# Other operation times in a planner: GpSimd's shifts, some of VectorE's operations, and when products of shifted copies count as ready

## The chip, the core and the metric

The kernel runs on one core of a Trainium2 chip. A core has a matrix engine (TensorE, PE in the profile), a vector engine (VectorE, DVE), an engine for activation functions (ScalarE, ACT), a general one (GpSimd, POOL) and one that issues transfers (SyncE, SP). Each works off its own instructions in the order of the program and waits on semaphores for the others. The metric is the device time of one execution in microseconds (us); of several executions the median is taken.

## The reference

Two attention layers over the same shapes (2048 positions, 512 channels, 32 heads of 16) stand side by side in the output: columns 0 to 511 are A, columns 512 to 1023 are B. Inputs are bfloat16.

```python
def _A_ref(x, wqkv, wo):          # linear attention
    q, k, v = qkv[0], qkv[1], qkv[2]            # of x @ wqkv, 32 heads of 16
    phi = lambda t: jnp.where(t > 0, t + 1, jnp.exp(t)) + 1e-6
    pq, pk = phi(q), phi(k)
    kv = jnp.einsum("bhsd,bhse->bhde", pk, v)
    z = jnp.einsum("bhsd->bhd", pk)
    num = jnp.einsum("bhqd,bhde->bhqe", pq, kv)
    den = jnp.einsum("bhqd,bhd->bhq", pq, z)[..., None] + 1e-6
    o = num / den
    return (lambda x, *d: x.transpose(*d))(o, 0, 2, 1, 3).reshape(B, S, D) @ wo

def _B_ref(x, wqkv, wo):          # softmax attention
    q, k, v = qkv[0], qkv[1], qkv[2]
    scale = Dh ** -0.5
    scores = jnp.einsum("bhqd,bhkd->bhqk", q, k) * scale
    p = _softmax(scores, axis=-1)
    o = jnp.einsum("bhqk,bhkd->bhqd", p, v)
    return (lambda x, *d: x.transpose(*d))(o, 0, 2, 1, 3).reshape(B, S, D) @ wo
```

Nearly all the work is B's 32 heads x 2048 x 2048 exponentials and the products on both sides of them.

## The kernel before

**Units and blocks.** B's work is cut into 32 units: four groups of eight heads, four chunks of 512 queries, and the even or the odd four heads of the group. In a unit, four heads lie in four row groups of TensorE. A unit has 64 blocks; a block is one head's scores of 128 keys by 512 queries, one product (line 809) with 32 rows. In all that makes 2048 blocks. The products of probabilities and values (line 1129) go to one PSUM bank, pPV, in four column groups of 17 columns (16 of the head, and one of ones for the sum); only one unit can have that bank at a time. When its last product is done, VectorE transposes the bank to OT (line 1229), takes the reciprocal of the sums (line 1240) and multiplies (line 1234).

**Two paths for a block.** A block goes through one of two paths.
- ScalarE: the scores stand in pS (five banks), two or three blocks together; one exponential (line 1010) writes PT, and one product per block follows.
- VectorE: the scores stand in pD (two banks, or one lent by pS). VectorE writes a 16-bit integer DI (line 911) whose bits, read as a float16, are a coarse exponential. Two shifted copies DJ are made of it (line 1081), each by adding a constant, by GpSimd or now and then by VectorE; a shift is for up to two blocks (1024 columns). The three copies, times values scaled by 1, 0.797 and 0.633 (the VV copies, line 625), add up to a finer exponential: three products per block, one from DI and two from DJ.

**A's work and the projections.** A's linear attention (88 jobs) and the projections of B's later groups are jobs of a few stages each (matrix products in a free pD bank, then VectorE, sometimes ScalarE). In A's phi, ScalarE writes the exponential EA (line 638), VectorE bounds it (line 647) and adds the positive part (line 640).

**What sets the order.** The kernel is written by a planner that runs while the kernel is built. It holds a clock for each engine (`T`) and a list of what could go next with its ready time and a cost in us written out in the code; again and again it takes what could start earliest, with priorities for near ties, moves that engine's clock by the cost, and adds the instruction to that engine's program. The costs leave no trace in the program but the order, the choice of path for a block, and the choice of engine for a shift; waits on the chip are by semaphores. The names that matter here:
- `d_pick` decides whether a block goes to VectorE: not if VectorE's planned queue is over `DBL` = 4.0 us, or GpSimd's over `PBL` us. GpSimd's queue is reckoned in `p_backlog`: its clock, and a cost for each shift that is still to come. Blocks that it doesn't take are left for ScalarE.
- `shift_cand` plans a shift: for GpSimd at `dp`, for VectorE at `dd`, both linear in the columns. VectorE is taken where GpSimd would end over `LM` us later. There are ten DJ buffers.
- `pv_cand` plans the products with values. A product may start when its probabilities are ready by the plan (`x[0]`; `x[2]` is 0 for PT and DI, 1 or 2 for the shifted copies); they go out in rounds of up to four, two rounds at once at most. `VHI` raises their priority when 24 are outstanding.
- `v4_job`, `phi_stages` and `unit_done` hold the stages with costs that the change touches (the VV copies, A's phi, the end of a unit).
- A's jobs have ready times spread evenly over the kernel, each moved by up to `JIT` = 6 us by a fixed hash of its number and `SEED`.
- `fill_idle` puts idle matmuls on FZ where the plan leaves TensorE idle over 0.25 us (eight in this kernel).

Of the kernel before, what the change touches and what calls it, by code (L numbers as in the profile page):

```python
# [12 lines left out]
ALU = mybir.AluOpType  # L13
# [222 lines left out]
def bass_concat_heads__linear_attn_block__softmax_full_mha__prompt_kernel(nc, A_x, A_wqkv, A_wo, B_x, B_wqkv, B_wo, out):  # L236
# [14 lines left out]
    UB = NT * 4  # L251
    PVB = 8
    PVW = 0.3
    NPP = 2
    DNEXT = 8
    DEND = 12
# [5 lines left out]
    ALAG = 30.0  # L262
    DLEAD = 0.8
    DBL = 4.0
    PBL = 8.0
    SHL = ("pool", "pool")
    LM = 4.0
    FU = 0.6
    SEED = 11
    JIT = 6.0  # L270
    LATE = 0.2
    DBAL = 1
# [17 lines left out]
    with es:  # L290
        block = es.enter_context(nc.Block())

        def sb(name, shape, dt):
            return es.enter_context(nc.sbuf_tensor(name, shape, dt))
# [20 lines left out]
        EA = sb("EA", [128, 2, 512], BF)  # L315
        OT = sb("OT", [128, 2, 512], F32)
        XN = OT.bitcast(BF)[:, 1, :].rearrange("p (x n) -> p x n", n=512)
        ZR = sb("ZR", [128, 2, 16], F32)
# [135 lines left out]
        tok = {}  # L454
# [54 lines left out]
        def f_op(lane, fn, reads=(), writes=()):  # L509
            return lambda bk: sch.add(lane, fn, reads=reads, writes=writes)  # L510
# [11 lines left out]

        def halves(fn, reads, n=4, parts=NPP, dur=MM, after=None, kind="f"):

# [84 lines left out]
        def v4_job(t4, Gp, lane="pool", **kw):  # L609
            sl = Gp % 2  # L610
            def mm(e, bk, i):
                tl, cc = divmod(i, 4)
                t = 4 * t4 + tl
                return e.matmul(f32v(bk)[:, tl * 128:(tl + 1) * 128], lhsT=xTb[:, cc, t * 128:(t + 1) * 128],
                                rhs=Wb[:, cc, 1024 + Gp * 128:1024 + Gp * 128 + 128], start=(cc == 0), stop=(cc == 3))
            ts = range(4 * t4, 4 * t4 + 4)
            def load_wo():
                load(WOb, wob, [("Wb", 2)])
            st = halves(mm, [("Wb", 2)] + [("xTb", t) for t in ts], n=16, parts=NPP, dur=0.06, after=load_wo if (t4, Gp) == (3, NGP - 1) else None)
            vv = lambda k: VV[:, sl, k, 4 * t4:4 * t4 + 4, :].rearrange("p t c -> p (t c)")  # L620
            st.append(("dve", 0.6, f_ev("dve", lambda e, bk: e.tensor_copy(  # L621
                VV[:, sl, 0, 4 * t4:4 * t4 + 4, :].rearrange("p t (h c) -> p t h c", c=17)[:, :, :, 0:16],
                f32v(bk).rearrange("p (t h d) -> p t h d", t=4, d=16)), [], [("VV", t, sl, 0) for t in ts])))
            for k in (1, 2):
                st.append((lane, 0.5 if lane == "dve" else 0.65, f_op(lane, lambda e, k=k: e.tensor_scalar(  # L625
                    vv(k), vv(0), SW[k], 0.0, op0=ALU.mult, op1=ALU.add),
                    [("VV", t, sl, 0) for t in ts] + [("VV1", sl)], [("VV", t, sl, k) for t in ts])))
            needs = ["WbV"] + [("xTb", t) for t in ts] + ([("pvdone", Gp - 2)] if Gp >= 2 else [])
            return Job(st, needs, [(k, ("V", Gp, t, k)) for k in range(3) for t in ts], rel=0, **kw)
# [4 lines left out]
        def phi_stages(x, ea, keys):  # L634
            q = ectr[0] % 2
            ectr[0] += 1
            E = ea(EA[:, q, :])
            ex = f_op("act", lambda e: e.activation(E, x, ACTF.Exp), keys, [("EA", q)])  # L638
            ex.buf = ("EA", q)
            add_ = f_op("dve", lambda e: e.scalar_tensor_tensor(x, x, 0.0, E, op0=ALU.max, op1=ALU.add),  # L640
                        [("EA", q)] + keys, keys)
            def last(bk):
                add_(bk)
                give_back(("EA", q), T["dve"])
            return [
                ("act", 0.52, ex),
                ("dve", 0.48, f_op("dve", lambda e: e.tensor_scalar(EA[:, q, :], EA[:, q, :], 1.0, 1e-6, op0=ALU.min, op1=ALU.add),  # L647
                                  [("EA", q)], [("EA", q)])),
                ("dve", 1.07, last)]

        def akv_job(t, hp, **kw):
            n = 4 * hp + t // 4
# [5 lines left out]
            def after():  # L658
                next_xa(n)
                if hp == 1 and t == NT - 1:  # L660
                    load(WOa, woa, ["WaV"])
            st = halves(mm, ["Wa", "WaV", ("xTa", n % 2)], n=8, parts=NPP, dur=0.11, after=after if t % 4 == 3 else None, kind="v")
            st.append(("dve", 0.6, f_ev("dve", lambda e, bk: e.tensor_copy(KV[:, t, 2:514],
# [170 lines left out]
        pend = []  # L834
# [10 lines left out]

        def p_backlog(at):
            w = max(0.0, T["pool"] - at) + sum(c_[3] for c_ in cands["pool"])
            w += 1.07 * len(pend)
            for s_ in dgroup["st"].values():
                if not s_.get("chained"):  # L850
                    w += 1.07 * len(s_["items"])
            return w

        def lagging(at):
# [208 lines left out]
        def shift_cand():  # L1063
            if not pend:
                return None
            buf, k, n, w, I, items, t_ = pend[0]
            jb = jn[0] % NDJ
            if jfree[jb] is None:
                return None
            dp, dd = 0.1 + w * 0.00095, 0.1 + w * 0.00045  # L1070
            sp, sd = max(T["pool"], vis("dve", t_), jfree[jb]), max(T["dve"], t_, jfree[jb])
            tp = sp + sum(c_[3] for c_ in cands["pool"]) + dp * len(pend)
            td = sd + sum(c_[3] for c_ in cands["dve"]) + dd
            ln, st_, d_ = ("dve", sd, dd) if tp > td + LM else ("pool", sp, dp)
            def run(st_, en_):
                pend.pop(0)
                jn[0] += 1
                jfree[jb] = None
                jleft[jb] = n
                J = DJ[:, jb, 0:w]  # L1080
                sch.add(ln, lambda e: e.tensor_scalar(J, I, 1.0, float(SH[k]), op0=ALU.mult, op1=ALU.add),  # L1081
                        reads=[("DI", buf, i) for i in range(n)], writes=[("DJ", jb)])
                for i, b in enumerate(items):
                    pv_ready[b[0]].append((vis(ln, en_), b, k, DJ.bitcast(F16)[:, jb, i * 512:(i + 1) * 512], ("DJ", jb), ("j", jb)))
                free_di(buf, vis(ln, en_))
            return st_, 0, ln, d_, run, None, "f"
# [4 lines left out]
        def pv_cand():  # L1091
# [1 line left out]
            if u >= NU or pvopen[0] is None:  # L1093
                return None
            Gp, c, e_ = unit(u)
            at = lambda x: max(x[0], tok[("V", Gp, x[1][1], x[2])])
            lst = [x for x in pv_ready[u] if ("V", Gp, x[1][1], x[2]) in tok]
            if not lst:
                return None
# [2 lines left out]
            if not rd:  # L1102
                x = min(lst, key=at)
# [13 lines left out]
            if len(rounds[0]) < 4 and not final and len(rd) < 8 and streaming(t_) > UT:  # L1117
                t_ += PVW
            def make(rounds):
# [102 lines left out]
        def unit_done(u, t_):  # L1222

            if u == NU - 1:
                return last_unit_done(u, t_)
            xb = (u // 2) % 2
            Gp, c, e_ = unit(u)
            lease("OT", 1)
            sch.add("dve", lambda e: e.transpose(OT[:, 0, :], PVb[:, 0:512]), reads=[("PV", g) for g in range(4)], writes=[("OT", 0)])  # L1229
            pvopen[0] = vis("dve", t_)  # L1230
            o = OT[:, 0, :].rearrange("p (b r) -> p b r", r=32)
            xn = XN[:, xb, :].rearrange("p (b r) -> p b r", r=32)
            zr = ZR[:, 0, 0:16]
            mul = f_op("dve", lambda e: e.tensor_tensor(xn[:, :, 16 * e_:16 * e_ + 16], o[:, :, 0:16],  # L1234
                                                        zr.unsqueeze(2).broadcast_to([128, 16, 16]), op=ALU.mult),
                       [("OT", 0), ("ZR", 0)], [("XN", xb, e_)])
            def norm(bk):
                mul(bk)
                give_back("OT", 0.0)
            st = [("dve", 0.2, f_op("dve", lambda e: e.reciprocal(zr, o[:, :, 16]), [("OT", 0)], [("ZR", 0)])),  # L1240
                  ("dve", 0.72, norm)]
            if e_ == 1:
                k = 4 * Gp + c
                st.append(("dve", 0.65, f_op("dve", lambda e: e.transpose(ON[:, k, :], XN[:, xb, :]), [("XN", xb, 0), ("XN", xb, 1)], on_keys(k))))
            urgent.append(Job(st, [("ot", u - 1)] if u else [], [(1, ("ot", u))] + ([(2, ("on", Gp, c))] if e_ == 1 else []),
                              bank=False, ready=t_, prio=0.5))
            if Gp == NGP - 1 and e_ == 1:
                for tl in range(4):
                    urgent2.append(omm_job("b", 4 * c + tl, tl, [("on", Gp, c)], [(-1, ("st", c, tl))]))
# [122 lines left out]
        while True:  # L1372
            opts = []
            for eng in T:
                best = None
                for c_ in cands[eng]:
                    st = max(T[eng], c_[0])
# [37 lines left out]
            o = min((o for o in opts if o[0] <= t0 + 0.03), key=lambda o: (o[1], o[0], -o[3]))  # L1415
            st, _, eng, dur, run_, c_, kind = o
# [25 lines left out]
        last = {}  # L1442
# [77 lines left out]
```

## Time and profile before

| | |
|---|---|
| median of three runs | 726.06 us (723.94 to 726.2) |
| the profiled execution | 725.82 us, span 723.8 us |
| granted clock of TensorE | 0.991 |
| busy: TensorE, ScalarE | 669.3 us, 680.5 us |
| busy: GpSimd, VectorE | 645.7 us, 641.1 us |
| exponentials (line 1010) | 654 instructions, 666.6 us |
| shifts (line 1081) | 581 on GpSimd, 39 on VectorE |

The span runs from the first to the last instruction on the core. A group's row in the profile gives line, engine, operation, output and input tile, shape and count, then busy time and the mean length of one in ns, then the time that its engine stood idle ahead of it and what ended most of that. A row of waits gives who waited, for whom, the time in all, how many times, and the longest. In a row of the timeline stand start and length in us, the instruction and, in brackets, the idle time ahead of it. Instructions of one engine may overlap in the records, so that a mean length can be over the time from start to start.

### The profile page before, as it was taken

What the parts mean: (1) busy time and instruction counts of PE and PEld (TensorE: products, weight loads), DVE (VectorE), ACT (ScalarE), POOL (GpSimd) and SP (SyncE); (2) the same over time, 40 slices, a digit from 0 to 9 for tenths busy, and PEclk for the clock granted to TensorE, in tenths of its full rate; (3) what the DMA queues carried; (4) which work ended last, traced back from release to release, by engine and by line L of the source; (5) the groups of instructions that cost most, each with busy time, mean ns of one, the idle gap of its engine ahead of it and who ended that gap; (6) DMA issues with size and microseconds to landing.
All of it is one profiled execution on the core that took longest, in us unless ns stands there. A gap on an engine that the chain in (4) does not pass through costs nothing.

```text
span 723.8 us, 19047 instructions
## 1 busy us (share of the span) xinstructions
PE 669.3 (92%) x8128; PEld 210.6 (29%) x8128; DVE 641.1 (89%) x1037; ACT 680.5 (94%) x692; POOL 645.7 (89%) x630
## 2 busy tenths in 40 slices
PE   7999999989998999899989998999988989899996
PEld 4323322323332333322222232222222222222222
DVE  6998899989997999888988988888999878989975
ACT  5899999989998998999999999999999999999995
POOL 7699999998999999989988999989999887999994
PEclk9999999999999999999999999999999999999999
DMA  9500011101001101020011001021000100021101
GB/s 208 143 2 2 9 30 32 37 9 39 2 2 31 31 2 31 1 68 12 13 31 37 16 1 30 3 59 38 8 9 9 38 24 31 1 38 31 30 31 34
DMA packets 54508, 21.75 MB, mean 30 GB/s; under 512 B 45200, under 2 KB 53904, under 8 KB 54416
## 3 DMA queue, kind: packets, MB, share of 16 engines
q1 hardware_dynamic: 53360, 20.20, 12.0%
q8 instruction: 66, 1.08, 0.6%
q10 hardware_dynamic: 1056, 0.26, 0.2%
q14 instruction: 26, 0.21, 0.1%
HBM read 4.19 MB, written 4.19 MB: 12 GB/s over the span
## 4 chain that ended last, share of the span: by engine, by line
POOL 49%; DVE 17%; PE 16%; ACT 12%; issue 4%; DMA 1%; DVEq 0%; POOLq 0%
POOL DJ L1081 47%; ACT PT L1010 12%; DVE DI L911 10%; PE pPV L1129 6%; PE pS L809 5%; PE pD L516 3%; POOL VV L625 2%; DVE OT L1229 1%; PE pS L516 1%; DVE DJ L1081 1%; DMA xTb<-in_B_x_dram 1%; DVE EA L647 1%; DVE PQT L640 1%; DVE VV L621 1%; PE pD L809 0%
## 5 line engine op out<-in xcount | busy, mean ns | idle before, releaser
L1010 ACT ACTIVATE PT<-pS 128x1024 f16<-128x1024 f32 (+1 forms) x654 | 666.6, 1180 | 28.9 <-PE pS L809 14.1
L1081 POOL TENSOR_SCALAR DJ<-DI 128x1024 int16<-128x1024 int16 (+1 forms) x581 | 622.5, 1073 | 65.9 <-DVE DI L911 19.2
L911 DVE TENSOR_SCALAR DI<-pD 128x512 int16<-128x512 f32 (+1 forms) x469 | 314.2, 688 | 38.7 <-PE pD L809 31.8
L809 PE MATMUL pS<-QT,KM 32*128 32x512 bf16 x1570 | 258.9, 386 | 14.6 <-ACT PT L1010 12.2
L1129 PE MATMUL pPV<-DJ,VV 128*17 128x512 f16 x1234 | 245.6, 386 | 24.3 <-POOL DJ L1081 23.0
L1129 PE MATMUL pPV<-PT,VV 128*17 128x512 f16 x1431 | 255.7, 385 | 1.6 <-DVE OT L1229 1.6
L809 PE MATMUL pD<-QT,KM 32*128 32x512 bf16 x478 | 171.4, 386 | 2.1 <-DVE DI L911 1.4
L1129 PE MATMUL pPV<-DI,VV 128*17 128x512 f16 x617 | 154.9, 385 | 2.3 <-DVE OT L1229 2.2
L809 PEld LDWEIGHTS pS<-QT,KM 32*128 32x128 bf16 x1570 | 63.9, 91 | 245.3 <-ACT PT L1010 179.5
L911 DVE TENSOR_SCALAR DI<-pS 128x512 int16<-128x512 f32 x139 | 93.9, 676 | 4.6 <-PE pS L809 3.7
L1129 PEld LDWEIGHTS pPV<-DJ,VV 128*17 128x17 bf16 x1234 | 52.1, 88 | 96.7 <-POOL DJ L1081 59.9
L1129 PEld LDWEIGHTS pPV<-PT,VV 128*17 128x17 bf16 x1431 | 53.1, 88 | 49.1 <-issue 41.5
L809 PEld LDWEIGHTS pD<-QT,KM 32*128 32x128 bf16 x478 | 40.6, 91 | 17.6 <-DVE DI L911 10.0
L1129 PEld LDWEIGHTS pPV<-DI,VV 128*17 128x17 bf16 x617 | 32.4, 88 | 24.8 <-issue 15.4
L516 PE MATMUL pD<-Wa,xTa 128*32 128x256 bf16 x896 | 34.8, 277 | 0.7 <-DVE DI L911 0.7
L516 PE MATMUL pD<-xTb,Wb 128*32 128x512 bf16 x432 | 31.3, 383 | 0.3 <-DVE DI L911 0.2
L1081 DVE TENSOR_SCALAR DJ<-DI 128x1024 int16<-128x1024 int16 x39 | 30.7, 791 | 0.0
L1229 DVE STREAM_TRANSPOSE OT<-pPV 128x512 f32<-128x512 f32 x31 | 21.9, 706 | 2.5 <-PE pPV L1129 2.5
L1234 DVE TENSOR_TENSOR OT<-OT,ZR 128x256 bf16<-128x256 f32 x31 | 23.5, 759 | 0.6
L516 PEld LDWEIGHTS pD<-Wa,xTa 128*32 128x32 bf16 x896 | 20.3, 97 | 12.8 <-issue 7.8
L520 DVE CAST KV<-pD 128x512 bf16<-128x512 f32 x24 | 16.4, 682 | 7.6 <-PE pD L516 7.6
L647 DVE TENSOR_SCALAR EA<-EA 128x512 bf16<-128x512 bf16 x32 | 22.3, 698 | 0.3 <-ACT EA L638 0.2
(109 smaller groups left out, 395.3 us busy)
## 6 DMA issues: line engine op xcount, KB each, us to landing
out_dram<-KV SPq DMA_DIRECT2D x32, 128.0 KB, 1.7
KM<-KR SPq DMA_DIRECT2D x96, 16.0 KB, 1.8
Wa<-in_A_wqkv_dram SPq DMA_DIRECT2D x1, 1024.0 KB, 6.1
Wb<-in_B_wqkv_dram SPq DMA_DIRECT2D x2, 384.0 KB, 4.5
Wb<-in_B_wqkv_dram SPq DMA_DIRECT2D x1, 512.0 KB, 4.7
Wa<-in_A_wqkv_dram SPq DMA_DIRECT2D x1, 512.0 KB, 6.8
Wa<-in_A_wo_dram SPq DMA_DIRECT2D x1, 512.0 KB, 5.0
Wb<-in_B_wo_dram SPq DMA_DIRECT2D x1, 512.0 KB, 3.8
```

What stands on the lines that cost most here:

```text
L516: ins = e.matmul(out[32 * g:32 * g + 32], lhsT=lhsT[:, 32 * g:32 * g + 32], rhs=rhs, start=start, stop=stop, tile_position=(0, 32 * g))
L520: return lambda e, bk: (e.tensor_copy(out_fn(), in_fn(bk)) if lane == "dve" else e.activation(out_fn(), in_fn(bk), ACTF.Copy))
L621: st.append(("dve", 0.6, f_ev("dve", lambda e, bk: e.tensor_copy(VV[:, sl, 0, 4 * t4:4 * t4 + 4, :].rearrange("p t (h c) -> p t h c", c=17 ...
L625: st.append((lane, 0.5 if lane == "dve" else 0.65, f_op(lane, lambda e, k=k: e.tensor_scalar(vv(k), vv(0), SW[k], 0.0, op0=ALU.mult, op1=A ...
L647: ("dve", 0.48, f_op("dve", lambda e: e.tensor_scalar(EA[:, q, :], EA[:, q, :], 1.0, 1e-6, op0=ALU.min, op1=ALU.add), [("EA", q)], [("EA", ...
L809: return e.matmul(dst, lhsT=KM[32 * g:32 * g + 32, Gp % 2, e_, j * 128:(j + 1) * 128], rhs=QT[32 * g:32 * g + 32, Gp % 2, c * 512:(c + 1) ...
L911: sch.add("dve", lambda e: e.tensor_scalar(DI[:, buf, i * 512:(i + n) * 512], f32v(DBANK[bi], 512 * n), ESC, EB, op0=ALU.mult, op1=ALU.add ...
L1010: sch.add("act", lambda e: e.activation(PT[:, row, c0:c0 + w], SCR[sl][:, 0:w], ACTF.Exp, scale=SC), reads=skeys(sl)[:len(bl)], writes=[(" ...
L1081: sch.add(ln, lambda e: e.tensor_scalar(J, I, 1.0, float(SH[k]), op0=ALU.mult, op1=ALU.add), reads=[("DI", buf, i) for i in range(n)], wri ...
L1129: sch.add("pe", lambda e, g=g, j=j, h=h, k=k, P=P, first=first, last_=last_: e.matmul(PVb[32 * g:32 * g + 17, 0:512], lhsT=VV[:, Gp % 2, k ...
L1229: sch.add("dve", lambda e: e.transpose(OT[:, 0, :], PVb[:, 0:512]), reads=[("PV", g) for g in range(4)], writes=[("OT", 0)])
L1234: mul = f_op("dve", lambda e: e.tensor_tensor(xn[:, :, 16 * e_:16 * e_ + 16], o[:, :, 0:16], zr.unsqueeze(2).broadcast_to([128, 16, 16]), ...
```

## The change

Only numbers of the planner change, and one condition: in `pv_cand` a product of a shifted copy counts as ready half a microsecond (`PVM`) after the copy. Planned operations: the shift on GpSimd (1024 columns: 1.073 us to 1.130 us) and on VectorE (0.561 to 0.701), the VV copies (VectorE 0.5 to 0.4, GpSimd 0.65 to 0.71), A's phi on VectorE (0.48 to 0.64 and 1.07 to 1.25), the reciprocal and the multiplication at a unit's end (0.2 to 0.26, 0.72 to 0.68). The limits `PBL` (8.0 to 6.5) and `LM` (4.0 to 5.0) and the number `SEED` (11 to 8) change too.

```diff
+    PVM = 0.5
...
-    PBL = 8.0
+    PBL = 6.5
     SHL = ("pool", "pool")
-    LM = 4.0
+    LM = 5.0
     FU = 0.6
-    SEED = 11
+    SEED = 8
...
-                st.append((lane, 0.5 if lane == "dve" else 0.65, f_op(lane, lambda e, k=k: e.tensor_scalar(
+                st.append((lane, 0.4 if lane == "dve" else 0.71, f_op(lane, lambda e, k=k: e.tensor_scalar(
...
-                ("dve", 0.48, f_op("dve", lambda e: e.tensor_scalar(EA[:, q, :], EA[:, q, :], 1.0, 1e-6, op0=ALU.min, op1=ALU.add),
+                ("dve", 0.64, f_op("dve", lambda e: e.tensor_scalar(EA[:, q, :], EA[:, q, :], 1.0, 1e-6, op0=ALU.min, op1=ALU.add),
                                   [("EA", q)], [("EA", q)])),
-                ("dve", 1.07, last)]
+                ("dve", 1.25, last)]
...
         def p_backlog(at):
             w = max(0.0, T["pool"] - at) + sum(c_[3] for c_ in cands["pool"])
-            w += 1.07 * len(pend)
+            w += 1.13 * len(pend)
             for s_ in dgroup["st"].values():
                 if not s_.get("chained"):
-                    w += 1.07 * len(s_["items"])
+                    w += 1.13 * len(s_["items"])
...
-            dp, dd = 0.1 + w * 0.00095, 0.1 + w * 0.00045
+            dp, dd = 0.157 + w * 0.00095, 0.22 + w * 0.00047
...
-            at = lambda x: max(x[0], tok[("V", Gp, x[1][1], x[2])])
+            at = lambda x: max(x[0] + (PVM if x[2] else 0.0), tok[("V", Gp, x[1][1], x[2])])
...
-            st = [("dve", 0.2, f_op("dve", lambda e: e.reciprocal(zr, o[:, :, 16]), [("OT", 0)], [("ZR", 0)])),
-                  ("dve", 0.72, norm)]
+            st = [("dve", 0.26, f_op("dve", lambda e: e.reciprocal(zr, o[:, :, 16]), [("OT", 0)], [("ZR", 0)])),
+                  ("dve", 0.68, norm)]
```

## The prediction

> **What bounds the kernel now.** I read the page's busy times and the chain of waits first, then the groups with shapes kept apart, then who waited for whom on each engine, and last short timelines. Busy time of the engines and the chain that ended last, from the page:
>
> ```profile
> span 723.8 us, 19047 instructions
> PE 669.3 (92%) x8128; PEld 210.6 (29%) x8128; DVE 641.1 (89%) x1037; ACT 680.5 (94%) x692; POOL 645.7 (89%) x630
> POOL 49%; DVE 17%; PE 16%; ACT 12%; issue 4%; DMA 1%; DVEq 0%; POOLq 0%
> ```
>
> Four engines are busy for about nine tenths of the span, and the chain changes from one to the other; half of it is GpSimd. The groups that the change prices or moves (count, busy us, mean ns of one, idle before):
>
> ```profile
> L1010 ACT ACTIVATE PT<-pS 128x1024 f16<-128x1024 f32 (+1 forms) x654 | 666.6, 1180 | 28.9 <-PE pS L809 14.1
> L1129 PE MATMUL pPV<-PT,VV 128*17 128x512 f16 x1431 | 255.7, 385 | 1.6 <-DVE OT L1229 1.6
> L1129 PE MATMUL pPV<-DI,VV 128*17 128x512 f16 x617 | 154.9, 385 | 2.3 <-DVE OT L1229 2.2
> L1129 PE MATMUL pPV<-DJ,VV 128*17 128x512 f16 x1234 | 245.6, 386 | 24.3 <-POOL DJ L1081 23.0
> L1081 POOL TENSOR_SCALAR DJ<-DI 128x1024 int16<-128x1024 int16 x575 | 618.8, 1077 | 65.5 <-DVE DI L911 19.2 <-PE pPV L1129 5.4
> L1081 DVE TENSOR_SCALAR DJ<-DI 128x1024 int16<-128x1024 int16 x39 | 30.7, 791 | 0.0
> ```
>
> Of the 2048 score blocks, 1431 go through ScalarE's exponential (one product each) and 617 through VectorE's integer form (one product from DI, two from the shifted copies DJ: 1234). A block on ScalarE costs 666.6 / 1431 = 0.466 us there. A block on VectorE costs one full-width shift on the average (575 + 39 of them, and six short ones, for 617 blocks).
>
> Who waited for whom (us in all, times, longest):
>
> ```profile
> ACT PT L1010 <- PE pS L809: 14.1, 21, 2.0
> ACT PT L1010 <- PE pD L809: 11.8, 22, 1.8
> ACT PT L1010 <- PE pD L516: 0.9, 1, 0.9
> PE pPV L1129 <- POOL DJ L1081: 23.0, 44, 2.0
> PE pPV L1129 <- DVE OT L1229: 3.8, 9, 1.6
> PE pD L516 <- DVE DI L911: 1.4, 6, 0.4
> PE pD L809 <- DVE DI L911: 1.4, 5, 0.3
> POOL DJ L1081 <- DVE DI L911: 19.2, 19, 2.7
> POOL DJ L1081 <- PE pPV L1129: 5.4, 2, 4.1
> ```
>
> ScalarE lost 14.1 + 11.8 + 0.9 = 26.8 us between exponentials, always to TensorE. What made TensorE late is seen in one stretch, around 221 us (start, length, instruction, idle before it):
>
> ```profile
> 215.79 9.01 POOL L1081 TENSOR_SCALAR DJ<-DI 128x1024 int16<-128x1024 int16 x8
> 221.47 0.38 PE L1129 MATMUL pPV<-DJ,VV 128*17 128x512 f16 x1 [1.94 <-POOL DJ L1081]
> 222.22 1.03 ACT L1010 ACTIVATE PT<-pS 128x1024 f16<-128x1024 f32 x1 [1.83 <-PE pD L809]
> 222.26 0.69 DVE L911 TENSOR_SCALAR DI<-pD 128x512 int16<-128x512 f32 x1 [2.17 <-PE pD L809]
> ```
>
> GpSimd runs without a gap; the product of a shifted copy stands in TensorE's queue before that copy exists; TensorE stands 1.94 us, and behind it, in program order, stand the score products for ScalarE and VectorE, which idle 1.83 and 2.17 us. The order had been written for a shift that ends earlier than it does.
>
> **The change part by part.** No instruction is of a new kind; the same planner gets other prices, so the order changes, and the share of blocks on each path.
>
> (a) GpSimd's shift of 1024 columns was planned at 0.1 + 1024 x 0.00095 = 1.073 us and is now planned at 0.157 + 0.973 = 1.130 us. What it takes from start to start is seen where GpSimd runs long without waiting:
>
> ```profile
> 338.90 30.96 POOL L1081 TENSOR_SCALAR DJ<-DI 128x1024 int16<-128x1024 int16 x27
> L1081 POOL TENSOR_SCALAR DJ<-DI x581: 620/1047/1474, 11.4 to 713.4; 128x1024 int16<-128x1024 int16 x191, 128x512 int16<-128x512 int16 x3
> ```
>
> 30.96 / 27 = 1.147 us. The plan was short by 0.074 us on each of 575, 42.6 us over the kernel, and is now short by 0.017, 9.8 us. (b) PVM lets the plan count a shifted copy's products ready 0.5 us later; the 44 waits for such copies average 23.0 / 44 = 0.52 us, so the margin is about one mean wait.
>
> What (a) and (b) can give back: of TensorE's waits for others than ScalarE in the list above (23.0 + 3.8 + 1.4 + 1.4 = 29.6), 23.0, or 78%, are for a shifted copy. I give them the same share of ScalarE's 26.8: 20.8 us, which is the upper bound; the lower is 0. If waits were spread exponentially with mean 0.52, a margin of 0.5 would remove 62% of their sum and the better price more; shifts that take up to 1.474 us beside a median of 1.047 stay unforeseen. I take three quarters: -15.6 us.
>
> The margin's own price: where the last products of a unit are put off, the single pPV bank turns later. There are 31 such turns before the last, so 0 to 31 x 0.5 = 15.5 us. TensorE lost only 3.8 us in 9 turns to that today, with score products and exponentials of the next unit ahead of it in the meantime; I take 0. Without that cover it would be the 15.5. A shifted copy also keeps its buffer 0.5 us longer; GpSimd waited for one only twice (5.4 us), off ScalarE's path: 0 to 5.4, taken as 0.
>
> (c) PBL from 8.0 to 6.5 with 1.13 for 1.07 a shift: a new block is sent to VectorE only while GpSimd's queue holds under 6.5 / 1.13 = 5.8 shifts, where it was 8.0 / 1.07 = 7.5. LM from 4.0 to 5.0: VectorE takes over a shift only when it would be done 5 us sooner. Both, and (a), send blocks from VectorE back to ScalarE at 0.466 us each. If the plan loads GpSimd as long as before, 575 becomes 575 x 1.073 / 1.130 = 546, 29 fewer; if VectorE also takes none of its 39, it is 68 blocks, +31.7 us. At the other end, GpSimd's own dry time of 19.2 + 5.4 = 24.6 us has room for 24.6 / 1.147 = 21 more blocks, -9.8 us. GpSimd delivered its 575 at the true 1.147, so an honest price need not cost all 29; but the shorter queue and the dearer takeover pull the same way. I take 22 fewer: +10.3 us. VectorE and GpSimd have fewer instructions by that, TensorE 44 fewer products; I count nothing for it.
>
> (d) The other new prices, by the groups with shapes apart:
>
> ```profile
> L647 DVE TENSOR_SCALAR EA<-EA 128x512 bf16<-128x512 bf16 x32 | 22.3, 698 | 0.3 <-ACT EA L638 0.2
> L640 DVE SCALAR_TENSOR_TENSOR KV<-KV,EA 128x512 bf16<-128x512 bf16 x16 | 19.6, 1227 | 0.1
> L640 DVE SCALAR_TENSOR_TENSOR PQT<-PQT,EA 128x512 bf16<-128x512 bf16 x16 | 19.3, 1204 | 0.1
> L1234 DVE TENSOR_TENSOR OT<-OT,ZR 128x256 bf16<-128x256 f32 x31 | 23.5, 759 | 0.6
> L1240 DVE RECIPROCAL ZR<-OT 128x16 f32<-128x16 f32 x31 | 7.2, 232 | 0.0
> L625 POOL TENSOR_SCALAR VV<-VV 128x544 bf16<-128x544 bf16 x24 | 16.1, 670 | 1.1
> ```
>
> They come closer to what is recorded (0.48 to 0.64 for 698 ns, 1.07 to 1.25 for 1227, 0.65 to 0.71 for 670, VectorE's shift 0.56 to 0.70 for 791). VectorE idles far more than this (723.8 - 641.1 = 82.7 us), so it hides them: 0; uncovered, the 64 slow ones of L647 and L640 would give at most 64 x 0.17 = 11 us back, which the 20.8 above already holds in part. (e) SEED deals the ready times of path A's 88 jobs anew, within 6 us each; instructions are the same. It can remove or double ScalarE's other waits, 26.8 - 20.8 = 6.0 us: between -6 and +6, taken as 0.
>
> **Sum**, against the profiled execution's 725.8 us (2.0 over its span; 0.2 under the median of 726.06): 725.8 - 15.6 + 10.3 = **720.5 us**. ScalarE would then be busy 680.5 + 10.3 = 690.8 us, 96% of it.
>
> One rule of the Trainium skill speaks against the first term. Rows first:
>
> ```profile
> 252.53 1.10 DVE L640 SCALAR_TENSOR_TENSOR KV<-KV,EA 128x512 bf16<-128x512 bf16 x1
> 253.17 1.36 POOL L1081 TENSOR_SCALAR DJ<-DI 128x1024 int16<-128x1024 int16 x1
> ```
>
> A shift that starts while L640 runs takes 1.36 us, 0.31 over the median. There are 32 of L640, so 32 x 0.31 = 9.9 us of GpSimd time comes in lumps that a mean price cannot place. The Trainium skill ("SBUF — State Buffer", section "Who interferes with whom") says that a VectorE instruction with two inputs in SBUF contends with a GpSimd one that reads SBUF, and that the later one is held up; the trace agrees, with these 0.31 us.
>
> **The rivals.**
> - R1, the ports: lateness is made by these lumps, not by the price. Then 9.9 us of the first term stay: 725.8 - 5.7 + 10.3 = 730.4. Against it: 0.31 us is inside the new margin of 0.5. (A mechanism of the rows above; the rule beside it is the one just named.)
> - R2, the wait only changes place: GpSimd is the true limit, a shift comes no sooner for being asked later, and ScalarE waits for score products or free PT rows in place of TensorE waiting for DJ. For it: the gapless 30.96 us. Against: then fewer blocks shorten the limit too. The first term is eaten to about the second, 10.3: 725.8, no change.
> - R3, slower: the queue limit in d_pick starves the VectorE path. It decides at 15.6 / 0.466 = 33 blocks: beyond, ScalarE's added work is over what the waits give. At 47 fewer (570 blocks): 725.8 - 15.6 + 21.9 = 732.1. For it: 5.8 shifts of cushion where GpSimd already ran dry 19 times. Against: those dry spells took only 19.2 us.
> - R4, more: all 20.8 us vanish, and 12 blocks move (+5.6), with path A's new order helping by half its bound (-3): 707.6; with the order neutral 710.6. I take 711. For it: 23.0 of TensorE's 29.6 us are of one kind.
>
> **How the numbers follow.** Forecast (716 to 724) 0.44; R4 (below 716) 0.15; R2 0.21; R3 0.13; R1 0.07. About 0.3% (2.2 us) is what a measurement of this kernel can tell from no change. Forecast, R4 and 0.01 of R2's lower edge are faster: 0.60. The rest of R2 is no change: 0.20. R1 and R3 are slower: 0.20. The likeliest one's own range is 716 to 724; to hold 8 in 10 I reach from R4's 711 to 731, between R1 and R3.
>
> **What would show each step.** TensorE's wait for DJ under 10 us with fewer than 25 times, and ScalarE's waits for TensorE near 11 us: the first term. PT products near 1453, DI products near 595, DJ shifts on VectorE under 39: the second. ScalarE busy near 691 us. The start-to-start time of shifts should stay at 1.147 us. If DI products are under 584, R3 decides; if the DJ waits fall and ScalarE's idle time does not, R2; if the remaining DJ waits stand behind L640, R1. I am wrong if the block shares hardly move, or if waits for OT at the units' turns take the place of those for DJ.

## The result, and the profile after

The changed kernel takes 705.6 us in the median of four runs (704.24 to 707.13) against 725.8 us, a ratio of 0.9727 with a 95% interval of 0.9699 to 0.9755: 2.7% faster. The forecast was 720.5 with a range down to 711; the time lies outside it, on the faster side. The profiled execution took 707.1 us.

Busy times and the chain of the page of after:

```profile
span 705.4 us, 18884 instructions
PE 662.9 (94%) x8086; PEld 206.5 (29%) x8086; DVE 616.8 (87%) x990; ACT 686.0 (97%) x694; POOL 634.6 (90%) x621
ACT 78%; POOL 7%; DVE 6%; PE 6%; DMA 1%; SPq 1%; issue 1%; ACTq 0%
```

The chain of waits, half of it GpSimd before, is now 78% ScalarE. Lines below the added `PVM = 0.5` (line 254) have moved down by one (line 1010 is now 1011, and so on). The groups that the prediction named:

```profile
L1011 ACT ACTIVATE PT<-pS 128x1024 f16<-128x1024 f32 (+1 forms) x656 | 675.5, 1326 | 5.0 <-PE pD L810 3.1 <-PE pS L810 1.5
L1130 PE MATMUL pPV<-PT,VV 128*17 128x512 f16 x1458 | 255.1, 384 | 0.0
L1130 PE MATMUL pPV<-DJ,VV 128*17 128x512 f16 x1180 | 230.5, 384 | 3.2 <-POOL DJ L1082 2.8
L1130 PE MATMUL pPV<-DI,VV 128*17 128x512 f16 x590 | 148.9, 384 | 1.7 <-DVE OT L1230 1.5
L1082 POOL TENSOR_SCALAR DJ<-DI 128x1024 int16<-128x1024 int16 x572 | 611.0, 1069 | 58.8 <-DVE DI L912 13.5
L1082 DVE TENSOR_SCALAR DJ<-DI 128x1024 int16<-128x1024 int16 x18 | 13.2, 734 | 0.0
```

590 blocks go through VectorE where it was 617, and 27 more through ScalarE; shifts are 572 on GpSimd (581 before) and 18 on VectorE (39). ScalarE's exponentials stand idle 5.0 us ahead of themselves where it was 28.9. Who TensorE waited for:

```profile
PE pS L810 <- ACT PT L1011: 21.1, 85, 0.7
PE pPV L1130 <- POOL DJ L1082: 2.8, 7, 0.7
PE pPV L1130 <- DVE OT L1230: 1.5, 3, 0.8
```

The 44 waits for a shifted copy (23.0 us) are 7 (2.8 us), and TensorE now stands longest for ScalarE, which is where the order wants it. These rows count products alone; TensorE's weight loads, which overlap with earlier products, waited 59.9 us (115 times) for shifted copies in before and 13.8 us (38 times) in after. ScalarE's own waits for TensorE fall from 26.8 us to 4.6 (3.1 + 1.5 in its row). GpSimd itself is not idler than before; a long stretch of its timeline:

```profile
238.44 45.11 POOL L1082 TENSOR_SCALAR DJ<-DI 128x1024 int16<-128x1024 int16 x39
```

45.11 / 39 = 1.157 us from start to start. Over all stretches of more than 25 us it is 1.147 us before (379 shifts) and 1.140 after (405 shifts): shifts come hardly sooner, but TensorE seldom stands waiting for them.

### The profile page after: what moved, and what is told of

It reads as the page before. It is cut to its first block, busy times and chain, and to the rows that moved or that the text cites. A ratio compares the mean times of both kernels' runs of the same rounds, so it can differ in the third digit from the quotient of the medians.

```text
span 705.4 us, 18884 instructions
## 1 busy us (share of the span) xinstructions
PE 662.9 (94%) x8086; PEld 206.5 (29%) x8086; DVE 616.8 (87%) x990; ACT 686.0 (97%) x694; POOL 634.6 (90%) x621
## 3 DMA queue, kind: packets, MB, share of 16 engines
q1 hardware_dynamic: 53360, 20.20, 12.5%
## 4 chain that ended last, share of the span: by engine, by line
ACT 78%; POOL 7%; DVE 6%; PE 6%; DMA 1%; SPq 1%; issue 1%; ACTq 0%
ACT PT L1011 76%; POOL DJ L1082 7%; DVE DI L912 3%; PE pPV L1130 2%; PE pS L810 2%; ACT EA L639 2%; PE pD L517 1%; DMA xTb<-in_B_x_dram 1%; SPq L368 1%; DVE VV L626 1%; DVE KMX L562 0%; PE pS L517 0%; DVE PQT L641 0%; DVE KM L560 0%; DVE EA L648 0%
## 5 line engine op out<-in xcount | busy, mean ns | idle before, releaser
L1011 ACT ACTIVATE PT<-pS 128x1024 f16<-128x1024 f32 (+1 forms) x656 | 675.5, 1326 | 5.0 <-PE pD L810 3.1
L1082 POOL TENSOR_SCALAR DJ<-DI 128x1024 int16<-128x1024 int16 x572 | 611.0, 1069 | 58.8 <-DVE DI L912 13.5
L912 DVE TENSOR_SCALAR DI<-pD 128x512 int16<-128x512 f32 (+1 forms) x476 | 320.6, 689 | 46.1 <-PE pD L810 40.8
L1130 PE MATMUL pPV<-DJ,VV 128*17 128x512 f16 x1180 | 230.5, 384 | 3.2 <-POOL DJ L1082 2.8
L810 PE MATMUL pD<-QT,KM 32*128 32x512 bf16 x484 | 175.0, 386 | 0.2 <-DVE DI L912 0.2
L1130 PE MATMUL pPV<-DI,VV 128*17 128x512 f16 x590 | 148.9, 384 | 1.7 <-DVE OT L1230 1.5
L912 DVE TENSOR_SCALAR DI<-pS 128x512 int16<-128x512 f32 x106 | 72.0, 679 | 4.2 <-PE pS L810 2.0
L810 PEld LDWEIGHTS pD<-QT,KM 32*128 32x128 bf16 x484 | 41.2, 91 | 13.5 <-DVE DI L912 6.0
L517 PE MATMUL pD<-Wa,xTa 128*32 128x256 bf16 x800 | 30.4, 274 | 0.0
L641 DVE SCALAR_TENSOR_TENSOR PQT<-PQT,EA 128x512 bf16<-128x512 bf16 x16 | 20.5, 1279 | 0.1
L641 DVE SCALAR_TENSOR_TENSOR KV<-KV,EA 128x512 bf16<-128x512 bf16 x16 | 17.7, 1109 | 0.1
```

The source lines that it names most:

```text
L517: ins = e.matmul(out[32 * g:32 * g + 32], lhsT=lhsT[:, 32 * g:32 * g + 32], rhs=rhs, start=start, stop=stop, tile_position=(0, 32 * g))
L810: return e.matmul(dst, lhsT=KM[32 * g:32 * g + 32, Gp % 2, e_, j * 128:(j + 1) * 128], rhs=QT[32 * g:32 * g + 32, Gp % 2, c * 512:(c + 1) ...
L912: sch.add("dve", lambda e: e.tensor_scalar(DI[:, buf, i * 512:(i + n) * 512], f32v(DBANK[bi], 512 * n), ESC, EB, op0=ALU.mult, op1=ALU.add ...
L1011: sch.add("act", lambda e: e.activation(PT[:, row, c0:c0 + w], SCR[sl][:, 0:w], ACTF.Exp, scale=SC), reads=skeys(sl)[:len(bl)], writes=[(" ...
L1130: sch.add("pe", lambda e, g=g, j=j, h=h, k=k, P=P, first=first, last_=last_: e.matmul(PVb[32 * g:32 * g + 17, 0:512], lhsT=VV[:, Gp % 2, k ...
```

## The experiments

Four theories were set against each other. P: GpSimd's shift was priced 0.074 us short, so that its planned clock ran ahead of the engine and its products stood too early in TensorE's queue; the price is the cause. M: the half-microsecond margin is. L: fewer blocks on GpSimd are. O: the new order of A's jobs is. A later one, V: a price too low on VectorE does the same there. The profiled executions and timed runs side by side (ratio to the kernel before, with its 95% interval; waits and busy time in us):

| kernel | ratio (interval) | TensorE's wait for DJ | idle ahead of exponentials | ScalarE busy | blocks on VectorE |
|---|---|---|---|---|---|
| before | 1 | 23.0 | 28.9 | 680.5 | 617 |
| after | 0.9727 (0.9699 to 0.9755) | 2.8 | 5.0 | 686.0 | 590 |
| b_short: order of before, shorter shifts | 0.9599 (0.9556 to 0.9642) | 1.3 | 6.5 | 674.2 | 617 |
| a_short: order of after, shorter shifts | 0.9668 (0.9629 to 0.9707) | none listed | 2.9 | 684.4 | 590 |
| b_price: the price alone | 0.9734 (0.9695 to 0.9773) | 3.9 | 7.7 | 678.7 | 607 |
| b_half: half the price's rise | 0.9793 (0.9764 to 0.9823) | 12.6 | 14.5 | 680.6 | 610 |
| b_over: a price past the truth | 0.9762 (0.9741 to 0.9784) | 0.3 | 13.0 | 683.1 | 601 |
| b_pvm: the margin alone | 0.9912 (0.9882 to 0.9941) | 14.2 | 16.8 | 684.2 | 601 |
| b_limits: PBL and LM alone | 1.0011 (0.9984 to 1.0037) | 21.0 | 20.3 | 687.3 | 596 |
| b_seed: SEED alone | 0.9955 (0.9926 to 0.9984) | 16.9 | 19.9 | 685.0 | 602 |
| a_no_price: all but the price | 0.9934 (0.9910 to 0.9959) | 17.6 | 15.5 | 689.6 | 590 |
| a_no_pvm: all but the margin | 0.9787 (0.9743 to 0.9832) | 3.7 | 3.6 | 689.9 | 579 |
| a_no_limits: all but PBL and LM | 0.9820 (0.9779 to 0.9862) | 0.3 | 10.4 | 682.7 | 600 |
| a_no_dve: all but VectorE's prices | 0.9826 (0.9804 to 0.9848) | 4.0 | 5.1 | 688.6 | 583 |
| b_over_dd: b_over, VectorE's shift dearer | 0.9812 (0.9787 to 0.9837) | none listed | 12.1 | 684.0 | 599 |
| best_1 | 0.9706 (0.9668 to 0.9743) | 2.6 | 7.4 | 680.0 | 609 |
| best_2 | 0.9722 (0.9694 to 0.9749) | 2.3 | 11.8 | 678.7 | 613 |

**The same order, and a shift that takes what the plan had said.** b_short changes no order and no price, but for one clearing of DJ by VectorE at the start. It makes the real operation shorter instead, and leaves the last 88 columns of each shifted copy out of the result.

```diff
+        sch.add("dve", lambda e: e.memset(DJ[:], 0), writes=[("DJ", j) for j in range(NDJ)])
...
+                c_ = min(w, 936)
-                sch.add(ln, lambda e: e.tensor_scalar(J, I, 1.0, float(SH[k]), op0=ALU.mult, op1=ALU.add),
+                sch.add(ln, lambda e: e.tensor_scalar(J[:, 0:c_], I[:, 0:c_], 1.0, float(SH[k]), op0=ALU.mult, op1=ALU.add),
```

> The order of before, instruction for instruction, but each full shift copies 936 of its 1024 columns (the last 88 of DJ keep the zeros that VectorE writes once at the start, so that part of the two shifted copies is left out of the result). By 0.83 ns a column that takes 0.073 us off each shift, which is just what the plan of before was short by. If the shift's price is the cause (theory P), TensorE's wait for DJ falls from 23.0 us to under 6, ScalarE's wait for TensorE from 26.8 to under 10, and the time to 700 to 708 us, with the 617 blocks on VectorE unchanged. If the cause is the number of blocks on GpSimd (theory L), the shorter shifts relieve it too, so L does not tell; if the order of the path-A jobs is the cause (theory O), the time stays over 720.

Measured: 696.1 us, ratio 0.9599, a little better than P's 700 to 708; O, which wanted over 720, is out here. The rows of b_short's groups and of its waits:

```profile
L1083 POOL TENSOR_SCALAR DJ<-DI 128x936 int16<-128x936 int16 (+1 forms) x581 | 579.4, 998 | 79.0 <-DVE DI L912 31.7
L1011 ACT ACTIVATE PT<-pS 128x1024 f16<-128x1024 f32 (+1 forms) x654 | 661.1, 1253 | 6.5 <-PE pS L810 4.7
```
```profile
PE pPV L1131 <- POOL DJ L1083: 1.3, 5, 0.6
```

A shift is 0.075 us shorter (998 for 1073 ns); in a stretch of 70 without a gap it takes 75.54 / 70 = 1.079 us from start to start, near the 1.073 of the plan. With the same 654 exponentials, the same blocks and the same order, 23.0 us of waits for DJ become 1.3 and ScalarE's idle time 28.9 becomes 6.5; of that its waits for TensorE go from 26.8 to 6.0. VectorE's 39 shifts are shorter too (704 ns for 791), 3.4 us in all, little beside the 29.7 us that the kernel gained. The same edit in the order of after (there `c_` stands in the same place):

> The order of after with the same short shifts (936 of 1024 columns, the rest of DJ stays zero and is left out of the result). By P the plan of after is already honest, TensorE waits only 2.8 us for DJ, and the time stays within 3 us of 705.6. If GpSimd's load were still what sets the time (L), 572 x 0.073 = 42 us less of it would give 10 us or more.

It gives 701.7 us, 3.9 under after, between the two expectations: P's 3 us is missed by 0.9, and L's 10 is far. The intervals of a_short and after overlap, so even the 3.9 are not clear of noise; in the order of before the same 0.075 us a shift was worth 29.7 us. GpSimd's dry time rises instead, from 13.5 us in after, in a_short's list of waits:

```profile
POOL DJ L1084 <- DVE DI L913: 56.3, 72, 5.7
```

**One part at a time, from the kernel before.** The price alone:

```diff
-            w += 1.07 * len(pend)
+            w += 1.13 * len(pend)
...
-                    w += 1.07 * len(s_["items"])
+                    w += 1.13 * len(s_["items"])
...
-            dp, dd = 0.1 + w * 0.00095, 0.1 + w * 0.00045
+            dp, dd = 0.157 + w * 0.00095, 0.1 + w * 0.00045
```

> Before with only GpSimd's shift priced at 0.157 + 0.00095 a column and 1.13 for 1.07 in the queue's reckoning; 607 blocks on VectorE, 554 shifts on GpSimd, 54 on VectorE. P: TensorE's wait for DJ falls under 10 us and the time to 703 to 712. Margin (theory M): the price alone leaves the products at the edge, the wait stays over 15 and the time over 715. L: 10 blocks fewer is a third of the way, 717 to 722.

Measured 706.1 us, ratio 0.9734, the same as the whole change within both intervals. The price stands in two places, the time of a shift and the queue's reckoning, and no run parts them; but b_limits, below, shortens that queue's limit by more than 1.13 for 1.07 does (8.0 to 6.5 us, where 1.07 / 1.13 makes 7.6 of 8.0) and gains nothing. b_price's wait for DJ:

```profile
PE pPV L1129 <- POOL DJ L1081: 3.9, 9, 0.8
```

The margin alone:

```diff
+    PVM = 0.5
...
-            at = lambda x: max(x[0], tok[("V", Gp, x[1][1], x[2])])
+            at = lambda x: max(x[0] + (PVM if x[2] else 0.0), tok[("V", Gp, x[1][1], x[2])])
```

> Before with only the half microsecond for products of shifted copies; 601 blocks on VectorE, 567 shifts on GpSimd. M: the wait for DJ falls under 8 us and the time to 703 to 712. P: the plan's GpSimd clock still runs ahead by 0.074 us a shift, a fixed half microsecond is used up after seven shifts in a row, the wait stays over 12 us and the time at 714 to 722. L: 16 fewer blocks, 712 to 718.

719.9 us: P's figures. In b_pvm's waits the fixed margin has taken less than half of them:

```profile
PE pPV L1130 <- POOL DJ L1082: 14.2, 34, 1.3
```

The limits alone (`PBL = 6.5`, `LM = 5.0`) and the seed alone (`SEED = 8`):

> Before with only PBL 6.5 and LM 5.0; 596 blocks on VectorE, 582 shifts on GpSimd, 14 on VectorE. L: fewer blocks relieve GpSimd, 708 to 714. P: GpSimd has as many shifts as before (582 for 581) at the old price, the wait for DJ stays at 18 us or more, 720 to 730.

> Before with only SEED 8; 602 blocks on VectorE, 570 shifts on GpSimd. O: 705 to 715. P: the price is unchanged, wait for DJ 18 us or more, 719 to 729; what lies under 725.8 is the 15 blocks fewer.

724.7 us, no change though 21 blocks had left VectorE; and 721.6 us, outside O's 705 to 715. Neither takes the wait away (first row b_limits, second b_seed), so O falls; P's figure for b_seed's wait, 18 us or more, was missed as well (16.9). b_limits says little of L, since GpSimd kept 582 shifts there; a_no_price, next, does.

```profile
PE pPV L1129 <- POOL DJ L1081: 21.0, 42, 1.1
```
```profile
PE pPV L1129 <- POOL DJ L1081: 16.9, 35, 1.3
```

**One part left out of after.** Without the price (`0.1 + w * 0.00095`, 1.07), and without the margin (`PVM = 0`):

> After with GpSimd's shift back at 0.1 + 0.00095 a column (and 1.07 in the queue's reckoning), all else of the change kept; 590 blocks on VectorE, as in after. P: the plan's GpSimd clock runs ahead again, the margin of 0.5 us covers part: wait for DJ over 10 us and 712 to 720 us. M: 703 to 708. L: the blocks are the same 590, so 705 to 707.

> After without the half microsecond; 579 blocks on VectorE. P: the wait for DJ stays under 10 us, and the time follows ScalarE's blocks, 705 to 711. M: wait for DJ over 15 us, over 714.

720.8 us without the price, with the very 590 blocks of after and 578 shifts on GpSimd for its 572: 15.2 us of the 20.2 are gone with it, and the DJ waits are back. That is 0.8 over P's 712 to 720 and far from L's and M's 703 to 708. Without the margin it is 709.7 us and the waits stay away (3.7 us in 10); its interval touches that of after, and 11 more blocks are ScalarE's there, so what the margin is worth stays open. a_no_price's wait:

```profile
PE pPV L1130 <- POOL DJ L1082: 17.6, 40, 1.1
```

**How much price.** Half the rise (0.128, 1.10), and more than a shift takes (0.217, 1.19), all else as in the kernel before:

> Before with half the rise of the price alone: the shift at 0.128 + 0.00095 a column, 1.10 in the queue's reckoning; 610 blocks on VectorE, 564 shifts on GpSimd. P: short by 0.046 us a shift where before is by 0.074, so the wait for DJ lies between 23.0 and 3.9 us, 11 to 16, and the time between 725 and 706, 713 to 719. If what counts is that a threshold is passed, the time is that of one end.

> Before with the price alone raised past what a shift takes: 0.217 + 0.00095 a column (1.190 us where 1.147 is measured), 1.19 in the queue's reckoning; 601 blocks on VectorE, 537 shifts on GpSimd, 67 on VectorE. P: nearly no wait for DJ (under 3 us) and nothing more to gain: 6 blocks more than with the right price on ScalarE, 705 to 712. If a later price goes on helping, under 703.

711.6 and 709.0 us. Half the rise leaves about half the waits for DJ; it gave some 14 of the 20 us, 1.4 more than I had set as its best. It is no threshold, then. Past the truth nothing more is gained: DJ waits are gone, but GpSimd runs dry and VectorE does 67 shifts. b_half's wait, and b_over's for GpSimd and for ScalarE:

```profile
PE pPV L1129 <- POOL DJ L1081: 12.6, 31, 1.6
```
```profile
POOL DJ L1081 <- DVE DI L911: 56.2, 55, 3.5
ACT PT L1010 <- PE pS L809: 8.2, 11, 2.4
ACT PT L1010 <- PE pD L809: 3.6, 7, 0.8
```

All of TensorE's waits that name VectorE add up to 12.9 us in b_over and 4.8 in after, which led to V. Three more kernels: b_over with `dd = 0.22 + w * 0.00047`, after with VectorE's prices of before (and GpSimd's for the VV copies), and after with `PBL = 8.0`, `LM = 4.0`.

> The kernel with the price past the truth (0.217, 1.19) and also VectorE's shift at 0.22 + 0.00047 a column; 599 blocks on VectorE, 63 shifts there. V: TensorE's waits for VectorE, some 11 us with the old price of that shift, fall under 6, ScalarE's wait from 11.8 to under 8, and the time to 703 to 707. Without V: within 2 us of 709.

> After with VectorE's prices (and GpSimd's for the VV copies) as before; 583 blocks on VectorE, 16 shifts there. P alone: these prices do nothing, and the 7 blocks that go to ScalarE make it 705 to 711. If a price too low on VectorE makes TensorE wait for VectorE as it does for GpSimd (theory V), TensorE's waits for DI, KV and OT together rise by 5 us or more, and it is 711 or over.

> After with PBL 8.0 and LM 4.0; 600 blocks on VectorE, 548 shifts on GpSimd, 54 on VectorE. P: honest prices and ten blocks fewer on ScalarE, 699 to 707; wait for DJ under 6 us. If the shorter queue is part of the gain, 709 or over.

b_over_dd is no better (711.0 us; TensorE's waits for VectorE 13.1 us), so the price of that one shift isn't what made VectorE late. a_no_dve is 711.4 us, as V has it. The waits for VectorE are up by 5.0 us (9.8 for 4.8), but those for DI, KV and OT, which V named, by 3.5 only (7.0 for 3.5), and ScalarE's idle time is 5.1 for 5.0; so V is not shown by it. a_no_limits is 709.5 us, just in the region that I had given to the shorter queue: ScalarE idles 10.4 us there, without waits for DJ. Each of these edits also deals the whole order anew, and with the right price, or more, the kernels with whole shifts lie between 703.4 and 711.4 us (ratios 0.971 to 0.983); with the old price they lie between 719.9 us and the time before (0.991 to 1.001), and b_half, with half the rise, is at 711.6 (0.979). Nothing was run that leaves SEED alone out of after. What parts those groups is the price; what lies within one I cannot put down to a single edit.

**Looking for a better one.** Both take the right price and leave VectorE's prices as before; best_1 has a margin of 0.25, `PBL = 7.0`, `LM = 4.0`, `SEED = 161`; best_2 has a price of 0.165 (1.138), no margin, `PBL = 9.0`, `LM = 5.0`, `SEED = 46`.

> The right price (0.157, 1.13), a margin of 0.25 us, PBL 7.0, LM 4.0, SEED 161, VectorE's prices as before; 609 blocks on VectorE. By P the time is then ScalarE's blocks and little more; two blocks fewer on ScalarE than with the price alone and a margin for the slow shifts: 698 to 706.

> A price nearer to the measured 1.147 (0.165 + 0.00095 a column, 1.138), no margin, PBL 9.0, LM 5.0, SEED 46, VectorE's prices as before; 613 blocks on VectorE, 60 shifts on VectorE. By P, with six blocks fewer on ScalarE than with the price alone: 697 to 705; the wait for DJ under 5 us.

703.4 and 706.6 us, the second 1.6 over what was expected. The intervals of both ratios (0.9706 and 0.9722) overlap with that of after: neither is shown to be better than after.

## Why the prediction was wrong

The cause that it named, shifted copies that come later than planned, is the right one, and so are most of its steps; its sum went wrong in the size of its first term. The profiled execution went from 725.8 to 707.1 us, 18.7 less, where the sum had 5.3 less. The 13.4 us between:

- **Wait given back: 6.6 us of it.** This is the step that failed: of ScalarE's 26.8 us of waits I gave 78% (20.8) to the shifted copies, called that the upper bound, and took three quarters, 15.6. The share itself held: in b_short, with no order changed, the waits fall to 6.0, and 20.8 us come back. The three quarters did not, and the bound did not either: in after the waits fall to 4.6, and 22.2 us come back. I had taken price and margin for one term and sized it by the margin. With the waiting spread as I had assumed, a margin of 0.5 leaves 38%; the margin alone did leave 14.2 of 23.0, 62%. The price alone left 3.9, because it removes the cause: 0.074 us short on each shift adds up in a long run of them.
- **Blocks moved: 4.8 us of it.** The count was near (590 for 595), and the price per block was too: b_short's 661.1 / 1431 is 0.462 us for the 0.466 that I had used, so 27 blocks cost 12.5 us. But ScalarE's busy time rose by 5.5 only, since the stalls had lengthened the busy time of before as well: with the same 654 exponentials it is 680.5 us in before and 674.2 in b_short. 674.2 + 12.5 = 686.7; measured 686.0. So 6.3 us more came back from the waits than the idle time shows, and the first term, taken as 15.6, was 22.2 + 6.3 = 28.5 us.
- **The rest, 2.0 us,** is what stays of the span without ScalarE's busy time and these waits, 723.8 - 680.5 - 26.8 = 16.5 us before and 705.4 - 686.0 - 4.6 = 14.8 after, and 0.3 us around the span.

Where do the 6.3 us hide? Just behind the stall that the prediction shows, the next instruction on ScalarE, in the timeline of before:

```profile
223.14 0.62 ACT L638 ACTIVATE EA<-KV 128x512 bf16<-128x512 bf16 x1
```

The exponential at 222.22 is recorded for 1.03 us, but its successor starts 0.92 us after it. A successor that is late loses this overlap before any idle time is counted: 0.11 us for each of ScalarE's 44 waits (21 + 22 + 1) is 4.8 us, near the 5.5 by which the exponentials' busy time differs between before and b_short (666.6 and 661.1). That this is all of it is argued, not shown.

The rivals. R4 (711, all 20.8 us vanish) was the nearest, still 3.9 us over the profiled 707.1, and that near only because its errors offset each other: it moved 12 blocks where 27 moved, and had nothing for the 6.3 us. R2 is out: the wait did not change place, since ScalarE's waits for TensorE fell to 4.6 us, and the chain is ScalarE's now. R3 is out: 27 blocks moved, not 33, and a_no_pvm with 38 moved is still 2.1% faster than before, so the point from which I had it decide was wrong as well. R1 is out as to its size: shifts of up to 1.42 us are still there, as the view of tile DJ in after has it, and the waits are 2.8 us where R1 kept 9.9.

```profile
L1082 POOL TENSOR_SCALAR DJ<-DI x572: 1044/1045/1420, 13.0 to 694.7; 128x1024 int16<-128x1024 int16 x191
```

For what is left R1 has the place right, though. Five of the seven waits in after, 1.9 us of the 2.8, come behind a shift of 1.36 or 1.38 us that began while L641 (L640 before) ran (in one case with another shift between), which was the sign set for R1. The lumps there are as the Trainium skill ("SBUF — State Buffer", section "Who interferes with whom") has them for a VectorE instruction with two inputs in SBUF beside a GpSimd one that reads SBUF.

The 1.147 us a shift are a mean that holds these lumps too. By the starts in the trace of before, the middle one of the 512 shifts that follow another without a wait (less than 0.2 us) comes 1.127 us after it, and their mean is 1.150. So the new price of 1.130 is that of the common shift, the old one was short by 0.054 us on it, and the rest of the 0.074 is slow shifts.

The smaller terms: the units' turns cost nothing (TensorE's wait for OT 3.8 to 1.5 us), as taken. SEED alone gave 0.45% (0.16 to 0.74), 3.3 us, within the 6.0 of its bound. VectorE's new prices were taken as 0; a_no_dve is 5.8 us slower than after in the median, which leaves open whether they are worth something in this order. Not all of them come closer to the records, as I had it: the multiplication went from 0.72 to 0.68 where 759 ns were recorded.

## What to carry to other kernels

Where a program's order is written ahead from assumed durations, compare each assumed duration with the time from start to start in a stretch without gaps, not with the length of a record; an error of 7% in the operation that runs without pause is an error that adds up, and the in-order engine that consumes its results carries it to all others. Here a fixed margin did not mend the drift, and a price past the truth gained nothing. When a stall's worth is estimated, the idle time that is shown is not the upper bound on an engine whose instructions overlap: here it was 22.2 us of 28.5.

## What the runs showed of the hardware

ScalarE's instructions overlap in the records, and more so the less they wait: the mean record of an exponential of 1024 columns is 1102 ns in before, 1175 in b_short with the same instructions, and 1231 in after (of 1536 columns: 1515, 1590, 1659). The busy time per block falls meanwhile, from 0.466 us to 0.462 and 0.463, and the idle time from 28.9 us to 6.5 and 5.0. So a longer record is no sign here of a slower engine. (The 1180 and 1326 in the rows above mix the two lengths, and after has more of the long ones, 146 for 124.)

GpSimd's shift was recorded at 1.077 us on the average of before, and the old price of 1.073 was just that; the 1.147 us from start to start hold 0.07 us more, which stand in no record and in no row of busy time. They stand in the idle time ahead of the shifts: of its 65.5 us in before only 19.2 + 5.4 name a cause, and the other 40.9 us are 0.071 for each of 575. I had not expected so little to decide 20 us of the kernel.
